# Attention, layer norm and two MLPs in one planned order: later landings and dearer POOL handovers in the planner, layer norm sums as float32r products

## The chip, the core and the metric

The kernel runs on one core of one Trainium2 chip. The core has a matrix engine (PE, with its weight loads, PEld), a vector engine (DVE), an activation engine (ACT), a general engine (POOL) and a queue that issues DMAs (SP). The metric is the device time in microseconds of one execution; lower is better. Float32r is the single-pass form in which PE reads 4-byte operands; a plain float32 product takes several passes.

## The reference, cut to what matters

```python
# attention per head: softmax(scale*q.k + min(bias from a cumulated s, 0), causal) @ v
x = attn_out.transpose(0, 2, 1, 3).reshape(B, S, H * D)          # B=4, S=576, 512 columns
mu = np.mean(x, axis=-1, keepdims=True)
var = np.mean((x - mu) ** 2, axis=-1, keepdims=True)
xn = (x - mu) / np.sqrt(var + 1e-06) * g_ln
x = x + np.maximum(xn @ w_ch1, 0.0) @ w_ch2                      # first MLP, 512 -> 2048 -> 512
u = x + ((x.transpose(0, 2, 1) @ U) @ V).transpose(0, 2, 1)      # mixing over the sequence, rank 32
out = u + np.maximum(u @ w2_ch1, 0.0) @ w2_ch2                   # second MLP
```

## The kernel before, in words

The work is cut into blocks: each of the four batches has a block A (256 positions) and a block B (320) for attention, layer norm and the first MLP, in the order A0 A1, A2 A3, B0, B1, B2, B3. The second MLP goes over C0, C1, C2 (512 positions of a batch each), T0 (the last 64 positions of all four batches) and C3. Nearly all products are float32r with operands split into a high and a low part, three products for one: L1396 to L1398 are the first half of the first MLP (and of T0), L1453 to L1455 its second half, L1309 to L1311 and L1347 to L1349 the two halves for C blocks. L765, L769 and L747 are attention's scores, L773 and L752 their reductions on DVE, L823 the transposes, L867 and L896 attention's second product. L1244 mixes T0's positions, one batch at a time.

Nothing is issued in the order of the text. Every step is recorded by `P.op` with its engines, a duration on each of them and its buffers, and `Plan.plan` places the steps one by one, earliest start first, on a model of the engines. What the model uses: `HOP`, the time from one engine's end to another's start; a DMA rate (350 bytes per ns) with 1500 ns from the queue's end to the reader, to which a load may add a `lag`; pools of buffers (`ps` six and `acc` two PSUM banks, `xs` two, `ls` four, `pB` two); and priorities from the tables `AT` (when a block's attention is spread over the MLP steps), `LN` (its layer norm), `W0`, `W1` (conversion of the second MLP's weights from 64-bit words) and `HEAD`. `Plan.issue` plans once from those priorities and then up to `PASSES` times from due times, and issues the order with the earliest planned end. Each engine then executes its own list strictly in that order, waiting on semaphores. So a step whose input comes later than the model says holds up everything behind it on its engine.

Where the plan leaves PE idle before the first MLP step, `issue` puts fillers there (L1603), short products into a bank that nobody reads.

The layer norm of a block (all but A0 and A1, which normalise by rows) sums over the 512 features, which lie on the partitions and in four tiles: `ln_sum` adds the four tiles (L386 on DVE or L388 on POOL, as the plan chooses) and then multiplies with a matrix of 1/512 to sum over the partitions and to spread the mean to all of them (L967). It is called twice a block, for the mean and for the variance:

```python
ps = psum()
pe(prio - 500, 4 * mm_cost(n), lambda: nc.tensor.matmul(ps[:, :n], ones.tile, into[:, :n], start=True, stop=True), [ones, into], [ps])
return ps
```

`split` takes a source and writes its high part (a copy with rounding to float32r, `copy`, on ACT or DVE: L381, L382) and its low part (source minus high part, `tt`, on DVE or POOL: L386, L388).

Of the kernel before, what the change touches and what calls it, by code (L numbers as in the profile page):

```python
# [10 lines left out]
F32R = mybir.dt.float32r  # L11
I32 = mybir.dt.int32
U32 = mybir.dt.uint32
AF = mybir.ActivationFunctionType
# [17 lines left out]
LAST = ("C0", "C1", "C2", "T0", "C3")  # L32
W2SLOTS = 12

AT = {"A2": (1, 3), "A3": (1, 33), "B0": (26, 49), "B1": (50, 65), "B2": (67, 83), "B3": (83, 100)}
LN = {"A2": 9, "A3": 33, "B0": 62, "B1": 66, "B2": 84, "B3": 102}
W0 = (1, 14)
HEAD = {-100: -1, -50: 127, 1.5: 61, 4.5: 18, -4: 1, -3: -8}
W1 = (16, 60, 59)
PASSES = 4  # L40
AHEAD = 1500


def f(ap):
    return ap.bitcast(F32)


def mm_cost(n):
    return max(106.7, n / 2.4) + 13.3


HOP = {
    ("pe", "act"): 200, ("pe", "dve"): 200, ("act", "pe"): 290, ("dve", "pe"): 285, ("pool", "pe"): 200,
    ("act", "dve"): 150, ("dve", "act"): 200, ("act", "act"): 150, ("dve", "dve"): 130, ("pool", "pool"): 100,
    ("act", "pool"): 170, ("dve", "pool"): 180, ("pool", "act"): 80, ("pool", "dve"): 80, ("pe", "pe"): 60,
}


# [30 lines left out]
class Plan:  # L89
# [196 lines left out]
    def issue(self, warm):  # L286
# [9 lines left out]
        for _ in range(PASSES):  # L296
            prio = self.latest(order, end)
            for o in self.ops:
                prio[o.seq] -= 1e3 * HEAD.get(o.prio, HEAD.get(o.prio + 500, 0))
            use = {e: [0.0] * NW for e in price}  # L300
# [35 lines left out]
def mha_ffn_mixer_ffn(ctx: ExitStack, tc, qkv_p, qkv_a, qkv_b, s, g, w1, w2, U, V, out):  # L336
    nc = tc.nc
    P = Plan(nc)
# [20 lines left out]
    def psum():  # L359
        return P.buf("ps", [128, 512])  # L360
# [6 lines left out]
    def act(prio, n, fn, reads, writes, fixed=94):  # L367
        P.op(prio, {"act": (fixed + 0.8333 * n, fn)}, reads, writes)

    def pe(prio, cost, fn, reads, writes, hold=()):  # L370
        return P.op(prio, {"pe": (cost, fn)}, reads, writes, hold=hold)
# [2 lines left out]
        return 4 * max(n / 2.4, 53.3) + 2.5  # L374

    def load(prio, nbytes, fn, reads, writes, gate=None, rate=350.0, lag=0):
        P.op(prio, {"sp": (475, fn)}, reads, writes, nbytes, gate, rate=rate, lag=lag)

    def copy(prio, n, out, a, reads, writes, psum=False, soft=0.0, slow=False):
        P.op(prio, {  # L380
# [10 lines left out]
    def split(prio, n, hi, lo, src, reads, wh, wl, psum=False, soft=0.0, slow=False):  # L391
        copy(prio, n, hi, src, reads, wh, psum, soft, slow)
        tt(prio, n, lo, src, lambda: f(hi()), ALU.subtract, list(reads) + list(wh), wl, psum, soft)


    def fixed(name, shape, dtype=F32):
        return P.fixed(const.tile(shape, dtype, name=name))

    ident = fixed("ident", [128, 128])
    ones = fixed("ones", [128, 128])  # L400
    eps = fixed("eps", [128, 1])
    odd = fixed("odd", [128, 1])
    g_sb = fixed("g_sb", [128, KT])
    small = fixed("small", [128, 4])
# [14 lines left out]
    PRO = -1e6  # L419

    def setup():
# [14 lines left out]
            dve(PRO, 1, lambda a=a, z=z: nc.vector.memset(odd[a:a + R], z), [], [(odd, "y%d" % a)])  # L436
        dve(PRO, 128, lambda: nc.vector.memset(ones.tile, 1.0 / DM), [], [ones], 0.521)
        P.op(PRO, {"pool": (600, lambda: nc.gpsimd.memset(causal.tile, 0.0))}, [], [causal])
        for y in range(4):
            act(PRO, R, lambda y=y: nc.scalar.activation(sel[R * y:R * (y + 1)], ident[R * y:R * (y + 1), R * y:R * (y + 1)], AF.Copy),  # L440
                [ident, table], [(sel, "y%d" % y)])
# [131 lines left out]
    def w2_ahead(m, gate):  # L573
        prio = NS0 + m - 8
        raw, t = w_raw(prio, 1, m, 1, gate, AHEAD), psum()
        f64_to_f32(prio, 512, lambda: t.tile, lambda: raw.tile, t, raw, psum=True)
# [3 lines left out]
    def w1_ahead(p, gate):  # L580
        prio, dr = NS0 + 2 * p - 9, w1_dr[p]
        raws, ts = [], []
        for z in range(2):
            raw, t = w_raw(prio, 1, 2 * p + z, 0, gate, AHEAD), psum()
            f64_to_f32(prio, 512, lambda t=t: t.tile, lambda raw=raw: raw.tile, t, raw, psum=True)
# [31 lines left out]
    class Pair:  # L617
# [94 lines left out]
        def bias(self, prio, tick, gate):  # L712
# [5 lines left out]
            for y in range(2):  # L718
                load(prio, 256 * S, lambda t=t, y=y: nc.sync.dma_start(
                    t[64 * y:64 * (y + 1)], cum_dr[idx + y:idx + y + 1].to_broadcast([64, S])), [cum_dr], [(t, "y%d" % y)], gate, 260.0, AHEAD // 2)  # L720
                d = lambda y=y: t[64 * y:64 * (y + 1), 512:S]
# [239 lines left out]
    def ln_sum(prio, n, srcs, reads, into):  # L961

        for k in range(1, KT):
            tt(prio, n, lambda: into[:, :n], srcs[0] if k == 1 else lambda: into[:, :n], srcs[k], ALU.add,
               (reads[0] if k == 1 else [into]) + reads[k], [into])
        ps = psum()
        pe(prio - 500, 4 * mm_cost(n), lambda: nc.tensor.matmul(ps[:, :n], ones.tile, into[:, :n], start=True, stop=True), [ones, into], [ps])  # L967
        return ps

    def layer_norm(prio, b, blk):  # L970
# [530 lines left out]
    for m in range(MT):  # L1501
        at = W1[0] + W1[1] * m / 8 if m < 8 else W1[0] + W1[1] + W1[2] * (m - 8) / 8
        if m % 2 == 0:
# [18 lines left out]
    for st in range(NS0, NS, 2):  # L1522
        _, _, blk, m = steps[st]
# [25 lines left out]
    put(start1 - 12, lambda p, g: mix_prep_v(p, g))  # L1549
    for x in AT:  # L1550
        b, blk = int(x[1]), x[0]
        if x not in FULL:
            for p, pr in enumerate(pairs_of[b, blk]):
                put(max(0, AT[x][0] - 6 + p), lambda p, g, pr=pr: pr.bounce(p, g))
        spread(attn_items(b, blk), *AT[x])
        put(LN[x], lambda p, g, b=b, blk=blk: layer_norm(p, b, blk))
    for (l, b, blk), p in final.items():
# [95 lines left out]
```

## Time and profile before

| what | value |
|---|---|
| median of 3 runs | 1037.3 us (1037.26 to 1037.39) |
| the profiled execution | 1036.19 us, span from first to last instruction 1034.4 us |
| granted TensorE clock | 1.0 of full speed, over the whole span |
| PE busy | 1017.1 us, 98% of the span |
| DVE, ACT, POOL busy | 694.6, 470.2, 138.5 us |
| DMA | 248.80 MB in the span, mean 241 GB/s |

The busy share of an engine counts the recorded instructions; the ends of matmuls are modelled, so that neighbours overlap in the records and the time that one matmul really takes is the distance from its start to the next one's.

### The profile page before, as it was taken

The numbers are of one execution on the slowest core, as the hardware profiler recorded it, in microseconds if no ns is written. First come the engines' busy times: TensorE is split into PE (matmuls) and PEld (weight loads), VectorE is DVE, ScalarE is ACT, GpSimd is POOL, SyncE is SP. The second block draws the span as 40 slices with busy tenths as digits, with TensorE's granted clock in tenths as the row PEclk, the third lists the DMA queues.
The fourth block names the chain that finished last, engine by engine and source line by source line (L and its number), as shares of the span: only waits on it lengthen the run. The fifth ranks groups of instructions, "written<-read, shape, count | busy, mean of one in ns | idle before, by whom it ended". The sixth has DMA issues, their size and how long they took to land.

```text
span 1034.4 us, 19312 instructions
## 1 busy us (share of the span) xinstructions
PE 1017.1 (98%) x7110; PEld 938.8 (91%) x7110; DVE 694.6 (67%) x1760; ACT 470.2 (45%) x1104; POOL 138.5 (13%) x288
## 2 busy tenths in 40 slices
PE   8999999999999999989999999999999999999998
PEld 7888888999999999979999999898999899899897
DVE  7999989866988878678754428547446645517444
ACT  6889877755856556557543314312111211112110
POOL 0021333511620222032100000001001000001000
PEclk9999999999999999999999999999999999999999
DMA  8999984668656976595475799981763576487851
GB/s 296 342 339 344 335 310 145 212 228 295 215 165 201 305 245 218 181 315 184 128 286 205 248 394 358 348 321 46 266 217 106 198 240 191 143 287 235 316 172 42
DMA packets 99231, 248.80 MB, mean 241 GB/s; under 512 B 16416, under 2 KB 47392, under 8 KB 94528
## 3 DMA queue, kind: packets, MB, share of 16 engines
q1 hardware_dynamic: 98464, 246.97, 69.6%
q8 instruction: 56, 0.92, 0.4%
q10 hardware_dynamic: 672, 0.59, 0.2%
q14 instruction: 39, 0.32, 0.1%
HBM read 193.97 MB, written 62.99 MB: 248 GB/s over the span
## 4 chain that ended last, share of the span: by engine, by line
PE 77%; DVE 5%; DMA 2%; ACT 2%; issue 1%; SPq 0%; DVEq 0%; POOL 0%; ACTq 0%; POOLq 0%
PE ps L1396 6%; PE ps L1398 5%; PE ps L1397 5%; PE ps L1309 5%; PE ps L1311 5%; PE ps L1310 5%; PE ps L867 4%; PE acc L1453 4%; PE acc L1454 4%; PE acc L1455 4%; PE ps L823 3%; PE acc L1347 3%; PE acc L1349 3%; PE acc L1348 3%; PE ps L1347 3%; PE ps L1348 3%
## 5 line engine op out<-in xcount | busy, mean ns | idle before, releaser
L1396 PE MATMUL ps<-xh,w 128*128 128x256 f32 (+1 forms) x512 | 157.8, 308 | 1.8 <-DVE pB L386 0.9
L1398 PE MATMUL ps<-xl,w 128*128 128x256 f32 (+1 forms) x512 | 151.3, 295 | 0.0
L1397 PE MATMUL ps<-xh,w 128*128 128x256 f32 (+1 forms) x512 | 151.2, 295 | 0.0
L1403 DVE SCALAR_TENSOR_TENSOR hl<-ps,hh 128x256 fp32r<-128x256 f32 (+1 forms) x144 | 64.5, 449 | 94.4 <-ACT hh L1402 94.0
L1402 ACT ACTIVATE hh<-ps 128x256 fp32r<-128x256 f32 (+1 forms) x144 | 58.2, 404 | 119.1 <-PE ps L1398 118.4
L1396 PEld LDWEIGHTS ps<-xh,w 128*128 128x128 f32 x512 | 96.7, 189 | 9.1 <-DVE pB L386 1.6
L1397 PEld LDWEIGHTS ps<-xh,w 128*128 128x128 f32 x512 | 96.8, 189 | 2.2
L1453 PE MATMUL acc<-hh,w 128*128 128x256 f32 (+1 forms) x320 | 97.3, 304 | 0.0
L1398 PEld LDWEIGHTS ps<-xl,w 128*128 128x128 f32 x512 | 96.6, 189 | 0.0
L1454 PE MATMUL acc<-hh,w 128*128 128x256 f32 (+1 forms) x320 | 93.8, 293 | 0.0
L1455 PE MATMUL acc<-hl,w 128*128 128x256 f32 (+1 forms) x320 | 93.8, 293 | 0.0
L1269 ACT ACTIVATE w<-hl 128x256 fp32r<-128x256 f32 x83 | 34.1, 418 | 124.7 <-DVE hl L1289 124.5
L783 ACT ACTIVATE t<-t,mx 128x384 f32<-128x384 f32 (+4 forms) x112 | 68.9, 617 | 47.0 <-DVE mx L773 39.2
L1289 DVE TENSOR_TENSOR hh<-ps,hh 128x256 f32<-128x256 f32 x64 | 27.1, 423 | 77.7 <-ACT hh L381 76.1
L1289 DVE TENSOR_TENSOR hl<-ps,hh 128x256 f32<-128x256 f32 x128 | 48.6, 419 | 44.9 <-PE ps L1311 43.7
L381 ACT ACTIVATE hh<-ps 128x256 f32<-128x256 f32 x31 | 12.0, 386 | 113.9 <-PE ps L1311 113.7
L386 DVE TENSOR_TENSOR pB<-ps,pB 128x384 fp32r<-128x384 f32 (+2 forms) x112 | 60.0, 569 | 5.2 <-ACT pB L381 4.7
L773 DVE CUSTOM_DVE_ANT_0 t<-ps,causal 128x128 f32<-128x128 f32 (+3 forms) x128 | 56.9, 484 | 8.5 <-PE ps L769 8.1
L1453 PEld LDWEIGHTS acc<-hh,w 128*128 128x128 f32 x320 | 60.7, 190 | 1.5 <-issue 1.0
L1454 PEld LDWEIGHTS acc<-hh,w 128*128 128x128 f32 x320 | 60.7, 190 | 0.5
L1455 PEld LDWEIGHTS acc<-hl,w 128*128 128x128 f32 x320 | 60.6, 190 | 0.0
L1295 DVE SCALAR_TENSOR_TENSOR w<-hl,w 128x256 fp32r<-128x256 f32 x128 | 52.3, 426 | 6.6 <-ACT w L1269 5.7
(258 smaller groups left out, 2894.8 us busy)
## 6 DMA issues: line engine op xcount, KB each, us to landing
w<-w_dr SPq DMA_DIRECT2D x112, 512.0 KB, 7.3
pB<-w_dr SPq DMA_DIRECT2D x36, 1024.0 KB, 5.4
qk<-w_dr SPq DMA_DIRECT2D x28, 768.0 KB, 5.2
w_dr<-w SPq DMA_DIRECT2D x32, 512.0 KB, 6.0
w_dr<-wr SPq DMA_DIRECT2D x32, 512.0 KB, 4.8
wr<-w1a SPq DMA_DIRECT2D x16, 512.0 KB, 6.3
wr<-w2a SPq DMA_DIRECT2D x16, 512.0 KB, 6.2
wr<-w1b SPq DMA_DIRECT2D x16, 512.0 KB, 6.5
```

Of the source, the lines that this page charges most:

```text
L386: alts = {"dve": (68 + 1.042 * n, lambda: nc.vector.tensor_tensor(out=out(), in0=a(), in1=b(), op=op))}
L783: act(prio, K, lambda t=t, mx=mx, o=o, K=K, x=x, y=nt * z + x: nc.scalar.activation(t[:, o:o + K], t[:, o:o + K], AF.Exp, bias=mx[:, (1 if ...
L1289: dve(st - 1000, 256, lambda: nc.vector.tensor_tensor(out=d.tile, in0=region(r), in1=a.tile, op=ALU.add), [p, a], [d])
L1347: nc.tensor.matmul(aa[z].tile, w[:, 0, sl], h[:, 0], start=first, stop=False)
L1348: nc.tensor.matmul(aa[z].tile, w[:, 1, sl], h[:, 0], start=False, stop=False)
L1396: nc.tensor.matmul(ps[:, :n], lhs(k, 0), xh[:, k, :n], start=k == 0, stop=False)
L1397: nc.tensor.matmul(ps[:, :n], lhs(k, 1), xh[:, k, :n], start=False, stop=False)
L1398: nc.tensor.matmul(ps[:, :n], lhs(k, 0), xl[:, k, :n], start=False, stop=k == KT - 1)
L1403: dve(st - 1000, n, lambda: nc.vector.scalar_tensor_tensor(out=hl[:, :n], in0=ps[:, :n], scalar=0.0, in1=f(hh[:, :n]), op0=ALU.max, op1=AL ...
L1453: nc.tensor.matmul(a, w[:, 0, sl], hh[:, :n], start=new, stop=False)
L1454: nc.tensor.matmul(a, w[:, 1, sl], hh[:, :n], start=False, stop=False)
L1455: nc.tensor.matmul(a, w[:, 0, sl], hl[:, :n], start=False, stop=last and (z == 1 or blk == "B"))
```

## The change

Three things change in the text. The planner takes every load with a priority above zero (all but those of the prologue and of the first block) to be read 1000 ns later than before (`LATE`); `HOP` from POOL to PE, ACT and DVE is 500 ns instead of 200, 80 and 80. The sum over partitions in `ln_sum` becomes a split of the added tile into two float32r parts and two float32r products with a float32r copy of the 1/512 matrix. And the tables `AT`, `LN`, `W0`, `HEAD` and `W1` have new numbers. Below line 400 the lines of the changed kernel stand a little further down: L967 becomes L975, L1396 L1407, L1244 L1255, L773 L776, L1463 L1474, L1603 L1614.

```diff
-AT = {"A2": (1, 3), "A3": (1, 33), "B0": (26, 49), "B1": (50, 65), "B2": (67, 83), "B3": (83, 100)}
+AT = {"A2": (1, 3), "A3": (1, 33), "B0": (26, 49), "B1": (46, 65), "B2": (69, 83), "B3": (83, 100)}
...
-W1 = (16, 60, 59)
+W1 = (16, 66, 56)
...
+LATE = 1000
...
-    ("pe", "act"): 200, ("pe", "dve"): 200, ("act", "pe"): 290, ("dve", "pe"): 285, ("pool", "pe"): 200,
+    ("pe", "act"): 200, ("pe", "dve"): 200, ("act", "pe"): 290, ("dve", "pe"): 285, ("pool", "pe"): 500,
...
-    ("act", "pool"): 170, ("dve", "pool"): 180, ("pool", "act"): 80, ("pool", "dve"): 80, ("pe", "pe"): 60,
+    ("act", "pool"): 170, ("dve", "pool"): 180, ("pool", "act"): 500, ("pool", "dve"): 500, ("pe", "pe"): 60,
...
-        P.op(prio, {"sp": (475, fn)}, reads, writes, nbytes, gate, rate=rate, lag=lag)
+        P.op(prio, {"sp": (475, fn)}, reads, writes, nbytes, gate, rate=rate, lag=max(lag, LATE if prio > 0 else 0))
...
+    mean_w = fixed("mean_w", [128, 128], F32R)
...
+        act(PRO + 1, 128, lambda: nc.scalar.activation(mean_w.tile, ones.tile, AF.Copy), [ones], [mean_w])
...
         ps = psum()
-        pe(prio - 500, 4 * mm_cost(n), lambda: nc.tensor.matmul(ps[:, :n], ones.tile, into[:, :n], start=True, stop=True), [ones, into], [ps])
+
+        parts = [P.buf("ls", [128, 320], F32R) for _ in range(2)]
+
+        def mm():
+            for z, a in enumerate(parts):
+                nc.tensor.matmul(ps[:, :n], mean_w.tile, a[:, :n], start=z == 0, stop=z == 1)
+
+        split(prio, n, lambda: parts[0][:, :n], lambda: parts[1][:, :n], lambda: into[:, :n], [into], [parts[0]], [parts[1]])
+        pe(prio - 500, 2 * mm_cost(n), mm, [mean_w] + parts, [ps])
         return ps
```

Over the whole program PE has the same matmuls in both orders, but for the 12 layer norm products, which become 24, and the fillers, 54 before and 60 now. Of the 12 new splits the order gives 10 high parts to ACT and 2 to DVE. Additions and subtractions that write an `ls` tile: 17 on POOL before, 27 now. The order of every engine is cut anew; three places follow.

**DVE, where the attention of B3 begins beside the layer norm of B2.** `v0` is the tile of the values, `xs0` the raw values that a DMA brings, the `ISA` rows on t0 and t1 the reductions of scores, which free `ps4` and `ps1` (before) or `ps0` and `ps4` (now). Before:

```order
L386 TENSOR_TENSOR xc0_6642<-xc0_6642,ls0_6728 128x320
L382 CAST xh0_6801<-xc0_6642 128x320
L382 CAST v0_6710<-xs0_6726 128x5x64
L386 TENSOR_TENSOR xl0_6806<-xc0_6642,xh0_6801 128x320
L386 TENSOR_TENSOR v0_6710<-xs0_6726,v0_6710 128x5x64
L773 ISA t0_6789,mx4_6815<-ps4_6787,causal_91 128x512
```

Of the change, the same reductions and, 24 rows further on, the same cast:

```order
L776 ISA t0_6812,mx4_6835<-ps0_6810,causal_92 128x512
L776 ISA mx4_6835 128x1
L776 ISA t1_6813,mx5_6846<-ps4_6811,causal_92 128x512
...
L755 ISA t2_6822,mx0_6942<-ps0_6852,t2_6822,mx0_6942 128x288
...
L383 CAST v0_6844<-xs0_6914 128x5x64
L1414 SCALAR_TENSOR_TENSOR hl2_6961<-ps4_6959,hh2_6960 128x320
```

The cast that waits for the landing stood ahead of the reductions and now stands behind them, and behind those of the pair's last scores (t2).

**DVE, where C0 begins.** The rows of x3 add B3's finished MLP to x and free the two accumulators and two `ps` banks; `wr` are tiles of the second MLP's weights in conversion. Before:

```order
L1463 TENSOR_TENSOR x3_7041<-x3_7041,acc0_8421 128x320
L534 SCALAR_TENSOR_TENSOR ps3_9066<-ps3_9066,wr1_8963 128x512
L1463 TENSOR_TENSOR x3_7041<-x3_7041,ps2_8422 128x320
L382 COPY wr2_9103<-ps3_9066 128x256
L386 TENSOR_TENSOR wr3_8943<-ps1_9041,wr3_8943 128x512
L1289 TENSOR_TENSOR hh1_9115<-ps4_9056,hh0_9054 128x256
L1463 TENSOR_TENSOR x3_7041<-x3_7041,acc1_8459 128x320
L1289 TENSOR_TENSOR hl2_9118<-ps4_9056,hh1_9115 128x256
L1463 TENSOR_TENSOR x3_7041<-x3_7041,ps0_8460 128x320
```

Of the change:

```order
L1474 TENSOR_TENSOR x3_7209<-x3_7209,acc0_8468 128x320
L387 TENSOR_TENSOR xs1_9121<-x1_8890,xs0_9045 128x512
L1300 TENSOR_TENSOR hh0_9131<-ps1_9062,hh2_9109 128x256
L383 CAST xh1_9139<-xs1_9121 128x512
L1474 TENSOR_TENSOR x3_7209<-x3_7209,ps4_8469 128x320
L387 TENSOR_TENSOR xh1_9139<-xs1_9121,xh1_9139 128x512
L1474 TENSOR_TENSOR x3_7209<-x3_7209,acc1_8494 128x320
L1300 TENSOR_TENSOR hh1_9165<-ps2_9123,hh0_9131 128x256
L1474 TENSOR_TENSOR x3_7209<-x3_7209,ps3_8495 128x320
```

The conversions of `wr` have left the stretch between the four additions; they come later in C0.

**PE, where T0 begins.** L1244 (now L1255) is the mixing of the fourth batch, with the operand t5 (now t3); L1347 to L1349 (now L1358 to L1360) are second-half products of C2; L1396 (now L1407) is T0's first product. Before, the last two mixing rows and on:

```order
L1244 MATMUL ps0_11719<-t0_8631,t5_11707 128x64
L1244 MATMUL ps0_11719<-t1_8642,t5_11707 128x64
L1347 MATMUL acc0_10984<-w0_11595,w1_11096 128x512
L1348 MATMUL acc0_10984<-w0_11595,w1_11096 128x512
...
L1348 MATMUL ps3_10999<-w0_11595,w1_11096 128x512
L1349 MATMUL ps3_10999<-w0_11595,w1_11096 128x512
L1396 MATMUL ps1_11751<-wr1_11735,pB0_11555 128x256
```

Of the change:

```order
L1359 MATMUL ps5_11067<-w5_11655,w9_11224 128x512
L1360 MATMUL ps5_11067<-w5_11655,w9_11224 128x512
L1255 MATMUL ps3_11818<-t0_8692,t3_11803 128x64
L1255 MATMUL ps3_11818<-t1_8696,t3_11803 128x64
...
L1407 MATMUL ps1_11838<-wr1_11829,pB0_11621 128x256
L1408 MATMUL ps1_11838<-wr1_11829,pB0_11621 128x256
```

Twelve products of C2 stood between the last mixing and T0's first product and none does now; between the third and the fourth mixing there were 6, and are 24 now. The low part of the fourth operand was made by DVE and is now made by POOL, and on SP the load for it stands behind one of T0's weight loads instead of ahead of it.

## Rows read from the trace of the kernel before

**Rows 1.** The page: busy time by engine; the chain that ended last.

```profile
PE 1017.1 (98%) x7110; PEld 938.8 (91%) x7110; DVE 694.6 (67%) x1760; ACT 470.2 (45%) x1104; POOL 138.5 (13%) x288
...
PE 77%; DVE 5%; DMA 2%; ACT 2%; issue 1%; SPq 0%; DVEq 0%; POOL 0%; ACTq 0%; POOLq 0%
```

**Rows 2.** Stretches: length, then busy PE, PEld, DVE, ACT, POOL; clock; DMA.

```profile
0.00:40.00 40.00, 35.79 (x292) 29.42 (x293) 33.52 (x136) 30.48 (x74) 2.13 (x12) 1.00 0.90 312
...
100.00:200.00 100.00, 97.92 (x713) 87.22 (x712) 90.77 (x234) 79.51 (x204) 35.18 (x66) 1.00 0.73 253
200.00:440.00 240.00, 239.70 (x1813) 228.06 (x1813) 187.54 (x471) 146.29 (x332) 56.52 (x132) 1.00 0.70 229
440.00:460.00 20.00, 17.08 (x119) 14.90 (x115) 14.76 (x36) 11.15 (x27) 8.62 (x17) 1.00 0.95 327
...
620.00:640.00 20.00, 18.68 (x132) 18.14 (x131) 15.91 (x31) 9.01 (x17) 1.30 (x1) 1.00 1.00 382
...
880.00:920.00 40.00, 37.88 (x273) 35.29 (x272) 16.24 (x38) 6.42 (x15) 0.00 (x0) 1.00 0.59 200
...
1020.00:1034.40 14.40, 10.49 (x55) 8.48 (x53) 5.68 (x17) 0.42 (x1) 0.00 (x0) 1.00 0.21 73
```

**Rows 3.** PE's waits, longest first: total us, times, longest.

```profile
PE ps L747 <- DVE mx L773: 2.0, 1, 2.0
...
PE ps L1309 <- DVE x L1463: 1.3, 1, 1.3
PE ps L1396 <- DMA pB<-w_dr: 1.3, 1, 1.3
...
PE ps L1396 <- DVE pB L386: 0.9, 1, 0.9
PE ps L1244 <- DVE t L386: 0.8, 1, 0.8
```

**Rows 4.** PE in time around one layer norm product: start, length, instruction.

```profile
331.36 0.70 PE L967 MATMUL ps<-ls,ones 128*128 128x320 f32 x2
331.66 0.55 PE L1453 MATMUL acc<-hh,w 128*128 128x320 f32 x1
332.04 0.31 PE L1454 MATMUL acc<-hh,w 128*128 128x320 f32 x1
332.19 0.31 PE L1455 MATMUL acc<-hl,w 128*128 128x320 f32 x1
```

**Rows 5.** SP, DVE and POOL in time, 437 to 447 us.

```profile
437.59 0.33 SPq L661 DMA_DIRECT2D xs<-qkv_b  x1
...
444.47 0.49 DVE L382 CAST v<-xs 128x320 fp32r<-128x320 f32 x1 [2.15 <-POOL xs L663]
...
445.39 1.10 POOL L388 TENSOR_TENSOR xc<-xc,ls 128x320 f32<-128x320 f32 x1
...
445.70 1.14 DVE L386 TENSOR_TENSOR v<-xs,v 128x320 fp32r<-128x320 f32 x1
446.76 0.68 DVE L773 CUSTOM_DVE_ANT_0 t<-ps,causal 128x512 f32<-128x512 f32 x1
```

**Rows 6.** DVE in time where C0 begins.

```profile
635.66 0.70 DVE L534 SCALAR_TENSOR_TENSOR ps<-ps,wr 128x512 uint32<-128x512 uint32 x1
...
639.02 0.48 DVE L1463 TENSOR_TENSOR x<-x,ps 128x320 f32<-128x320 f32 x1
```

**Rows 7.** DVE in time behind the fourth mixing of T0.

```profile
892.24 0.42 DVE L1247 TENSOR_TENSOR wr<-wr,ps 128x256 f32<-128x256 f32 x1 [0.71 <-PE ps L1244]
892.69 0.50 DVE L382 CAST wr<-wr 128x256 fp32r<-128x256 f32 x2
```

**Rows 8.** Groups by shape: xcount | busy us, mean ns | idle before.

```profile
L388 POOL TENSOR_TENSOR ls<-ls,ls 128x320 f32<-128x320 f32 x1 | 0.9, 883 | 3.3 <-ACT ls L981 3.3
...
L386 DVE TENSOR_TENSOR ls<-ls,ls 128x320 f32<-128x320 f32 x11 | 5.3, 484 | 0.1
```

**Rows 9.** PE in time, fillers before the first MLP step.

```profile
20.66 2.13 PE L1603 MATMUL acc<-ones 128*128 128x256 bf16 x18
```

More of the change, by code (lines that the diff above doesn't have):

```diff
@@ L33 @@
 W2SLOTS = 12
-AT = {"A2": (1, 3), "A3": (1, 33), "B0": (26, 49), "B1": (50, 65), "B2": (67, 83), "B3": (83, 100)}
-LN = {"A2": 9, "A3": 33, "B0": 62, "B1": 66, "B2": 84, "B3": 102}
-W0 = (1, 14)
-HEAD = {-100: -1, -50: 127, 1.5: 61, 4.5: 18, -4: 1, -3: -8}
-W1 = (16, 60, 59)
+AT = {"A2": (1, 3), "A3": (1, 33), "B0": (26, 49), "B1": (46, 65), "B2": (69, 83), "B3": (83, 100)}
+LN = {"A2": 9, "A3": 33, "B0": 63, "B1": 66, "B2": 84, "B3": 106}
+W0 = (1, 16)
+HEAD = {-100: -1, -50: 125, 1.5: 61, 4.5: 33, -4: 1, -3: -8}
+W1 = (16, 66, 56)
 PASSES = 4
 AHEAD = 1500
+LATE = 1000
 def f(ap):
```

## Prediction

> **What bounds the kernel now.** I read the page first. PE is busy 98% of the span and the chain that ended last runs over PE for 77% of it, with DVE next at 5% [rows 1]. PE is the bound, so the time is PE's own work plus whatever PE waits; the other engines matter only where they make it wait. The span is 1034.4 us and PE's busy time 1017.1, so 17.3 us are idle. The stretches tell where [rows 2]: 40 - 35.79 = 4.2 us in the first 40 us, 2.1 between 100 and 200, 2.9 between 440 and 460, 1.3 between 620 and 640, 2.1 between 880 and 920, and 3.9 in the last 14.4 us, most of it behind the last product. That is 16.5 of the 17.3; the long stretches between lose almost nothing. PE's waits name the events in the middle [rows 3]: 2.0 us for DVE's score reductions, 1.3 for DVE's addition L1463, 1.3 for a landing of `pB`, 0.9 for DVE's `pB`, 0.8 for a `t`.
>
> The profiled execution took 1036.2 us, 1.1 less than the median of 1037.3; differences worked out in its rows are put on the median.
>
> **Layer norm products.** What a float32 product costs is read from PE's starts [rows 4]. L967's first record starts at 331.36, the next engine's work at 331.66: 0.30 us. That next product then runs 0.38 us to its successor (332.04) where the one after takes 0.15 (332.19 - 332.04), so 0.23 of L967 is still in the array. One product of 320 columns costs 0.30 + 0.23 = 0.53 us. Two float32r products of 320 columns cost 2 x 0.147 = 0.29 by the same rows. Saved: 0.24 us, eight times (two sums in each of four B blocks), 1.9 us. The four products of 256 columns I scale by columns, an estimate: 0.19 each, 0.8 us. **Term: -2.7 us.** All 12 stand between products of the MLP with no idle time beside them, so it is PE's own time; bounds -2.2 to -2.9.
>
> The price is 12 splits, 12 copies and 12 subtractions. A 320-column addition in `ls` takes 0.484 us on DVE and 0.883 on POOL [rows 8]. The norm of a block is planned well ahead of its MLP (by the table `LN`, B1's at step 66, while B1's MLP begins at step 80, and 14 steps are 14 x 24 products of 0.147 us, some 49 us), so the longer chain of some 2 us a norm, two copies and two subtractions, is covered. What is not covered is DVE's time between 100 and 200 us, where it is busy 90.8 of 100 us [rows 2] and where the norms of A2 and A3 lie: by the order DVE gets 3 more `ls` operations of 256 columns there, 0.39 us each scaled from 0.484, 1.2 us. **Term: +0.3**, nearer to nothing because PE idles only 2.1 us there although DVE is that full; bounds 0 and +1.2.
>
> **Landings.** `LATE` and `HOP` change no transfer; they change what is put in front of what. At 437.59 SP issues a load of `xs`; DVE waits 2.15 us with the cast that reads it until 444.47; the score reduction behind the cast starts at 446.76 [rows 5], and PE needs the bank that it frees: the wait of 2.0 us [rows 3]. In the new order that cast stands 24 rows behind the same reductions, and behind those of the next scores. A landing just as late then holds up nothing that PE needs soon. **Term: -2.0**, and of the 0.9 us that PE waits a little later for DVE's backlog, half: **-0.5**. Bounds 0 and -2.9.
>
> **Where C0 begins.** PE's 1.3 us end with the last of the four L1463 at 639.02 [rows 6], which frees a bank. Before it stood two conversions (L534, 0.70 each) with their copy and subtraction, some 2.5 us. The new order has none of these there. **Term: -1.3**, bounds 0 and -1.3. They come later in C0, where DVE has slack (15.9 of 20 us even in the full stretch).
>
> **Where T0 begins.** Two waits go: the 0.8 us for the `t` (24 products of C2, not 6, now stand ahead of the fourth mixing) and perhaps the 1.3 for `pB`, because more second-half products of T0 are placed before each new weight tile. One comes: nothing of C2 is left between the fourth mixing and T0's first product. From the addition's start at 892.24 to the first cast's end at 892.69 + 0.25 is 0.7 us [rows 7]; with handovers of 0.2 to 0.3 at both ends and the low parts arriving one by one I take 1.5 us. The fourth operand is also made by POOL, with its load behind 1 MB of weights: +0.4. Together -2.1 + 1.9 = **-0.2**; bounds -2.1 (all covered) and +2.5.
>
> **The head.** Six more fillers at 2.13 / 18 = 0.12 us [rows 9] are 0.7 us of PE. They fill waiting that the plan expects; I take **+0.4**, bounds -1.0 and +1.5, since the 4.2 idle us of the head depend on an order that is new throughout. The copy for `mean_w` (one ACT operation) ends long before the first norm.
>
> **The rest of the order** is cut anew as well. I put its other waits at what they were, **0**, bounds -2 and +3.
>
> Sum: -2.7 + 0.3 - 2.5 - 1.3 - 0.2 + 0.4 + 0 = -6.0 us. The profiled execution would take 1030.2 us, the median **1031.3**.
>
> **A rule weighed.** DVE's subtraction at 445.70 took 1.14 us, beside a POOL addition that started at 445.39 and took 1.10 [rows 5]; a DVE addition of that size alone takes 0.484 [rows 8]. So 0.66 us of DVE were lost to POOL. The Trainium skill (SBUF — State Buffer, Who interferes with whom) says that DVE, with two inputs in SBUF, and a POOL instruction that reads SBUF exclude each other for a whole instruction; that row agrees. By that rule the change is worse than it looks, since it moves additions to POOL. What it would give is the second rival.
>
> **Rivals.**
> *The waits only move.* The plan is blind to what it was blind to before, and the 9 us that PE idles between head and tail come back at other places. Against it stand the two places in DVE's order at which the cause is seen to be gone. Then only the norm products (-2.7) and the fillers (+0.7) remain: 1035.3 us.
>
> *POOL holds DVE (slower).* POOL gets 27 of the `ls` operations instead of 17. Ten more at 0.66 us of DVE each are 6.6 us. If DVE passes all of that to PE, and the waits of the landings return elsewhere, the time is 1037.3 - 2.7 + 6.6 = 1041.2. It is slower by more than 0.2% from the point where 4.8 of these 6.6 us reach PE (2.7 gained, 2.1 for the 0.2%). For it: the score reductions behind such a held DVE row made PE wait. Against it: between 200 and 440 us DVE is busy 187.5 of 240 us and PE idle 0.3 [rows 2], so DVE has room there.
>
> *T0's beginning costs its upper bound.* The fourth operand comes 2.7 us later than I take it: 1031.3 + 2.7 = 1034.0, still faster.
>
> **How the numbers follow.** About 0.2% (2 us) is what a measurement here can tell from no change. Chances: the forecast with its bounds 0.60, T0's late beginning 0.10, waits that only move 0.16, POOL holding DVE or as much lost otherwise 0.14. The second last gives 1035.3, at the edge of 2 us. So faster 0.70, within 0.2% 0.16, slower 0.14. Adding all good ends (-2.9 - 2.9 - 1.3 - 2.1 - 1.0 - 2) gives 1025.1, all bad ones (-2.2 + 1.2 + 2.5 + 1.5 + 3) 1043.3; neither is likely in all its terms at once. I take 1026.0 to 1039.0, which leaves out the tip of the good side and the worst of the POOL case. Within the forecast alone it is 1027.5 to 1034.5.
>
> **What will show it.** Layer norm: two records of about 0.15 us pitch and no slow successor. Landings: no wait of L747 (now L750) near 440 us; if DVE still idles there for `xs`, but PE does not, the step is right. C0: no wait for L1474. T0: a new wait of 1 to 2 us of L1407 for DVE or ACT right behind L1255. Head: PE's idle time in the first 40 us within 1.5 us of 4.2. The prediction is wrong if PE's idle time between 40 and 1020 us stays at the 9.2 us of before (17.3 - 4.2 - 3.9), or if the head loses more than 2 us.

## The result and the profile after

The changed kernel takes 1026.2 us (median of 4 runs, 1025.4 to 1027.1), the kernel before 1037.3 beside it: a ratio of 0.9892, 95% interval 0.9875 to 0.9909, so 11.1 us or 1.1% faster. The forecast was 1031.3. The sign was right, and PE lost most of its idle time at the places that were named; the size was half of what came. The 1026.2 lie at the very edge of the stated range (1026.0 to 1039.0) and outside the 1027.5 to 1034.5 that the forecast alone allowed.

In the profiled execution the span falls from 1034.4 to 1024.3 us. The page of the changed kernel, busy time by engine and the chain that ended last (as [rows 1]):

```profile
PE 1013.0 (99%) x7116; PEld 937.3 (92%) x7116; DVE 691.4 (67%) x1763; ACT 476.3 (47%) x1122; POOL 146.8 (14%) x292
...
PE 86%; DVE 7%; DMA 4%; ACT 2%; issue 1%; POOLq 0%; SPq 0%; DVEq 0%; ACTq 0%; POOL 0%
```

PE's busy time fell by 1017.1 - 1013.0 = 4.1 us and its idle time from 17.3 to 1024.3 - 1013.0 = 11.3, by 6.0. Stretches as in [rows 2] (length, then busy PE, PEld, DVE, ACT, POOL; clock; DMA), the last one from 920 us on:

```profile
0.00:40.00 40.00, 36.62 (x311) 30.63 (x312) 35.25 (x139) 33.70 (x82) 2.13 (x12) 1.00 0.94 332
...
100.00:200.00 100.00, 99.06 (x740) 89.15 (x739) 87.93 (x232) 76.15 (x199) 34.46 (x62) 1.00 0.76 257
200.00:440.00 240.00, 238.64 (x1799) 226.08 (x1798) 190.22 (x474) 152.44 (x352) 60.29 (x137) 1.00 0.65 217
440.00:460.00 20.00, 20.00 (x143) 19.45 (x142) 15.68 (x42) 13.68 (x32) 5.21 (x11) 1.00 0.98 332
...
620.00:640.00 20.00, 19.85 (x141) 18.72 (x141) 19.97 (x46) 11.50 (x23) 1.67 (x1) 1.00 0.76 276
...
880.00:920.00 40.00, 38.60 (x300) 37.12 (x299) 10.26 (x25) 5.97 (x15) 1.29 (x1) 1.00 0.68 246
920.00:1020.00 100.00, 99.79 (x654) 90.76 (x653) 51.06 (x128) 16.07 (x37) 3.07 (x2) 1.00 0.53 188
```

PE's idle time (length less busy time), before and after: 4.2 and 3.4 us in the head, 2.1 and 0.9 from 100 to 200, 0.3 and 1.4 from 200 to 440, 2.9 and none from 440 to 460, 1.3 and 0.15 where C0 begins, 2.1 and 1.4 where T0 begins. Of these only the one from 200 to 440 grew, and 0.2 us came behind 920. PE's waits (as [rows 3]):

```profile
PE acc L1614 <- DVE ones L439: 1.5, 1, 1.5
PE ps L1407 <- DVE wr L383: 0.8, 1, 0.8
PE ps L1407 <- DVE hl L1414: 0.6, 1, 0.6
PE ps L1407 <- DVE mx L776: 0.5, 1, 0.5
PE ps L1407 <- DMA pB<-w_dr: 0.5, 1, 0.5
PE ps L768 <- DVE w L387: 0.5, 1, 0.5
```

Behind the start (1.5, as before) nothing is longer than 0.8 us, and that one is the new wait at T0's beginning which the prediction announced. The waits of 2.0, 1.3, 1.3 and 0.9 us of [rows 3] are gone, or 0.5. Between the head and the tail, PE idles some 4 us (0.9 + 1.4 + 0.15 + 1.4 + 0.2) where it idled 9.2.

### The profile page after: what moved, and what is told of

Same layout as the page of the kernel before. It is cut to its first block, busy times and chain, and to the rows that moved or that the text cites. A ratio compares the mean times of both kernels' runs of the same rounds, so it can differ in the third digit from the quotient of the medians.

```text
span 1024.3 us, 19382 instructions
## 1 busy us (share of the span) xinstructions
PE 1013.0 (99%) x7116; PEld 937.3 (92%) x7116; DVE 691.4 (67%) x1763; ACT 476.3 (47%) x1122; POOL 146.8 (14%) x292
## 4 chain that ended last, share of the span: by engine, by line
PE 86%; DVE 7%; DMA 4%; ACT 2%; issue 1%; POOLq 0%; SPq 0%; DVEq 0%; ACTq 0%; POOL 0%
PE ps L1407 7%; PE ps L1409 7%; PE ps L1408 7%; PE ps L1320 5%; PE ps L1322 5%; PE ps L1321 5%; PE ps L870 4%; PE acc L1464 4%; PE acc L1466 3%; PE acc L1465 3%; PE ps L826 3%; PE acc L1358 3%; PE acc L1359 3%; PE acc L1360 3%; PE ps L1358 3%; PE ps L1359 3%
## 5 line engine op out<-in xcount | busy, mean ns | idle before, releaser
L1407 PE MATMUL ps<-xh,w 128*128 128x256 f32 (+1 forms) x512 | 158.0, 309 | 1.9 <-DVE hl L1414 0.6
L1407 PEld LDWEIGHTS ps<-xh,w 128*128 128x128 f32 x512 | 96.6, 189 | 10.4 <-issue 2.8
L776 DVE CUSTOM_DVE_ANT_0 t<-ps,causal 128x256 f32<-128x256 f32 (+3 forms) x128 | 56.4, 485 | 10.8 <-PE ps L772 10.5
```

Of the source, the lines that this page charges most:

```text
L1407: nc.tensor.matmul(ps[:, :n], lhs(k, 0), xh[:, k, :n], start=k == 0, stop=False)
```

## The experiments

Twelve kernels ran. Each ratio is to the kernel before on the same chip; the changed kernel's own is 0.9892. The last column is the median.

| kernel | ratio (95%) | us |
|---|---|---|
| after_ln_fp32 | 0.9907 (0.9894 to 0.9920) | 1026.8 |
| after_no_ln | 1.0057 (1.0042 to 1.0071) | 1042.8 |
| after_no_late | 1.0083 (1.0063 to 1.0102) | 1043.8 |
| after_old_hop | 1.0051 (1.0037 to 1.0065) | 1041.4 |
| before_cast | 0.9993 (0.9982 to 1.0005) | 1035.7 |
| before_c0 | 1.0015 (1.0003 to 1.0026) | 1038.1 |
| before_lnr | 0.9986 (0.9972 to 1.0000) | 1034.7 |
| before_three | 1.0005 (0.9990 to 1.0019) | 1036.6 |
| before_far | 0.9994 (0.9976 to 1.0012) | 1036.4 |
| after_ls_dve | 0.9952 (0.9934 to 0.9970) | 1032.6 |
| after_late990 | 0.9894 (0.9875 to 0.9914) | 1026.9 |
| after_old_tables | 0.9935 (0.9916 to 0.9953) | 1030.7 |

The medians of before beside them were 1036.4 to 1036.9.

Where two kernels have the same order on PE, their records can be laid side by side, each with the same instruction of the other. The table gives how much later (us) PE starts the instruction that the first of the two starts at the time in the head line; each from one profiled execution of either.

| later than | kernel | 40 | 100 | 200 | 300 | 440 | 520 | 620 | 660 | 880 | 920 | 1015 |
|---|---|---|---|---|---|---|---|---|---|---|---|---|
| changed | after_ln_fp32 | 1.7 | 1.7 | 1.6 | 1.1 | 1.6 | 1.5 | 2.0 | 2.0 | 2.0 | 1.2 | 1.2 |
| changed | after_ls_dve | 2.2 | 2.2 | 3.6 | 6.1 | 7.0 | 7.3 | 7.3 | 7.3 | 7.3 | 6.5 | 6.5 |
| before | before_cast | 0.2 | -0.4 | 0.3 | 0.2 | 1.0 | 0.2 | 0.2 | 0.2 | 0.2 | 0.5 | 0.5 |
| before | before_c0 | -1.3 | -1.6 | -1.7 | -1.7 | -1.5 | -2.3 | -2.3 | 0.6 | 0.6 | 0.2 | 0.2 |
| before | before_lnr | -0.9 | -1.0 | -0.7 | -0.7 | -0.1 | -0.3 | -0.8 | -1.1 | -1.1 | -0.5 | -0.5 |
| before | before_three | -1.3 | -1.8 | -1.1 | -1.4 | 1.4 | -0.6 | -1.1 | 1.7 | 1.7 | 1.0 | 1.0 |
| before | before_far | -0.6 | -1.1 | -0.8 | -1.0 | -0.4 | -2.0 | -2.5 | 0.7 | 0.8 | -0.5 | -0.5 |

None of these kernels changes anything in the first 40 us but for a small operation that makes weights (before_lnr, before_three, before_far). So the head differs by up to 2 us from one execution to the next, and an edit is read from the step at its own place. Steps of some 0.9 us come without any edit: before_c0 changes nothing between 440 and 520 us, and PE gains 0.9 there.

### The price of the products: after_ln_fp32 and before_lnr

Both keep the order of all engines. after_ln_fp32 goes back to float32 in the changed kernel:

```diff
-            for z, a in enumerate(parts):
-                nc.tensor.matmul(ps[:, :n], mean_w.tile, a[:, :n], start=z == 0, stop=z == 1)
+            a = parts[0]
+            nc.tensor.matmul(ps[:, :n], ones.tile, f(a[:, :n]), start=True, stop=True)
```

> Changed kernel with its order kept row for row on DVE, ACT, POOL and SP, but each pair of float32r products of the layer norm sums replaced by one float32 product of the high part alone (the low part of the sums is left out). So only PE's price of the sums is changed back. By the term of the prediction (0.53 us for a float32 product of 320 columns against 0.29 for the pair, eight times, and 0.19 us for each of four of 256 columns): 2.7 us slower than the changed kernel, 1028.9 us, bounds 2.2 to 2.9. Rival: the products lie where PE would wait anyway, so that their price is not PE's own time: 0 to 1 us slower.

Around one of the sums, PE in time, start, length and instruction; first the changed kernel:

```profile
428.61 0.46 PE L975 MATMUL ps<-ls,mean_w 128*128 128x320 f32 x2
428.90 0.31 PE L1464 MATMUL acc<-hh,w 128*128 128x320 f32 x1
429.05 0.31 PE L1465 MATMUL acc<-hh,w 128*128 128x320 f32 x1
```

then after_ln_fp32:

```profile
429.65 0.70 PE L975 MATMUL ps<-ls,ones 128*128 128x320 f32 x2
429.95 0.56 PE L1464 MATMUL acc<-hh,w 128*128 128x320 f32 x1
430.35 0.30 PE L1465 MATMUL acc<-hh,w 128*128 128x320 f32 x1
```

The pair takes 428.90 - 428.61 = 0.29 us. The float32 product takes 0.30 and delays its successor to 0.40 where 0.15 is the pitch: 0.55 in all. That is the prediction's reading of [rows 4], measured again. PE's busy time is 1015.1 us, 2.1 more than in the changed kernel. But from 100 to 620 us, where all the sums lie, PE falls back by only 2.0 - 1.7 = 0.3 us, and the medians differ by 0.5 (the ratios by 1.5, with intervals that overlap; by the ratios alone the 2.7 of the term are not excluded). The changed kernel waits where this run does not: the waits of 0.6 for `hl` and 0.5 for `mx` in the list above are not in this run.

before_lnr does the opposite in the kernel before, without the splits:

```diff
-        pe(prio - 500, 4 * mm_cost(n), lambda: nc.tensor.matmul(ps[:, :n], ones.tile, into[:, :n], start=True, stop=True), [ones, into], [ps])
+        def mm():
+            for z in range(2):
+                nc.tensor.matmul(ps[:, :n], mean_w.tile, into[:, :n], start=z == 0, stop=z == 1)
+
+        pe(prio - 500, 4 * mm_cost(n), mm, [ones, into], [ps])
```

> Kernel before with its order kept, but each layer norm sum's float32 product made two float32r products of the sum rounded to float32r (the sums are rounded at each addition and there is no low part, so no split on DVE or POOL; one extra DVE operation at the start makes the weights). This is PE's price of the change alone. By the term of the prediction: 2.7 us faster than before, bounds 2.2 to 2.9. By the run of the changed kernel with float32 products, which cost it far less than 2.7 (medians 0.5 apart, ratios 1.5): 0.5 to 1.6 us faster, because a part of the time given back is spent waiting for DVE a little later.

The ratio of 0.9986 is 1.5 us (0 to 2.9), which does not exclude the term either. The records show where the time goes. Laid beside the kernel before, PE gains 0.2 to 0.3 us at each of the eight sums of 320 columns and some 0.2 at each of the four of 256, as the prediction priced them. It gives 1.6 us back between 346 and 353 us, where it now idles 0.6 + 0.4 us for DVE (none before), and the rest in smaller steps: between 40 and 880 us it gains 0.1.

```profile
345.86 0.66 PE L753 MATMUL ps<-qk 128*128 128x288 f32 x3 [0.60 <-DVE mx L779]
353.09 1.15 PE L829 MATMUL ps<-ident,t 128*128 128x128 f32 x6 [0.41 <-DVE mx L758]
```

### Two rows moved by hand: before_cast, before_c0, before_three, before_far

These keep the order of the kernel before and move a few operations (numbered as they are made) behind a later one, with whatever between depends on them. before_cast:

```diff
+        for names, goal in [((2605, 2606), 2614)]:
+            k = next(i for i, c in enumerate(best) if c[0].seq == goal)
+            late = [i for i, c in enumerate(best) if c[0].seq in names]
+            moved = set()
+            for i in range(min(late), k + 1):
+                o = best[i][0]
+                if o.seq in names or any(d.seq in moved for d in o.deps) or any(d.seq in moved for d in o.slots):
+                    moved.add(o.seq)
+            best = ([c for c in best[:k + 1] if c[0].seq not in moved] + [c for c in best[:k + 1] if c[0].seq in moved] + best[k + 1:])
```

> Kernel before with its order kept, but two DVE rows moved: the cast and the subtraction that wait for the landing of xs near 440 us stand behind the two score reductions (and behind the next 1/sum, an ls subtraction and an hl) instead of ahead of them. Theory of the prediction: 2.0 to 2.9 us faster than before, no wait of L747 near 440. Rival (PE waits for the next thing): the wait goes, but a new one near it takes its place, 0 to 1 us faster.

Less than the theory's 2.0 us is gained (the interval ends at 1.9), as the rival had it. By the records it is 0.75 us between 440 and 520, no more than before_c0 gains there without an edit. In before_cast (lines numbered 10 higher than before), DVE in time near 440 us:

```profile
444.56 0.69 DVE L783 CUSTOM_DVE_ANT_0 t<-ps,causal 128x512 f32<-128x512 f32 x1 [0.75 <-PE ps L779]
...
448.29 0.47 DVE L392 CAST v<-xs 128x320 fp32r<-128x320 f32 x1
...
451.47 0.46 DVE L762 CUSTOM_DVE_ANT_0 t<-ps,t 128x288 f32<-128x288 f32 x1 [0.78 <-DMA t<-cum_dr]
```

and PE's waits there:

```profile
450.38 0.52 PE L833 MATMUL ps<-ident,t 128*128 128x128 f32 x3 [0.78 <-DVE rc L802]
453.21 1.09 PE L833 MATMUL ps<-ident,t 128*128 128x128 f32 x8 [1.43 <-ACT t L808]
454.77 0.41 PE L1406 MATMUL ps<-xh,w 128*128 128x320 f32 x1 [0.47 <-DVE pB L396]
```

The reductions start 2.2 us earlier than the 446.76 of [rows 5], and the wait of 2.0 is gone. PE then runs into the next landing: the reduction L762 waits until 451.47 for `t` from `cum_dr`, the softmax's `t` is late by as much, and PE idles 0.78 + 1.43 + 0.47 = 2.7 us in the stretch, 2.9 before. In the kernel before, SP issues those two loads of `t` from 440.45 on, and in before_cast from 441.79. In the changed kernel SP issues them at 434.21, and the first of those reductions runs at 446.57, without a wait. So in this run the next late results, one of them a landing, take the place of the one whose row DVE waited in.

before_c0 has `[((3366, 3369, 3362), 3524)]` in the same place.

> Kernel before with its order kept, but three DVE rows moved: the conversion L534, its copy and the subtraction that stand between the four L1463 where C0 begins now stand behind the last of them. Theory of the prediction: 1.3 us faster than before, no wait of L1309 for L1463 over 0.2 us. Rival: C0 then waits for the converted weights instead, 0 to 0.5 us faster.

It is 1.6 us slower by the ratio (0.3 to 2.7), so both theory and rival were wrong. By the records PE is 2.3 us ahead at 620 us, up to which nothing is changed, and loses 2.9 between 620 and 660. PE in time:

```profile
636.70 0.39 PE L1319 MATMUL ps<-xc,pB 128*128 128x256 f32 x1 [0.79 <-DVE x L1473]
...
639.33 0.47 PE L1319 MATMUL ps<-xl,qk 128*128 128x256 f32 x1 [1.66 <-DVE hl L1299]
```

The wait for the addition shrank from 1.3 to 0.8; behind it PE now waits 1.7 us for C0's `hl`, in front of which the conversions stand, 0.66 us of that while DVE waits for ACT's half of a conversion. And the granted clock fell (stretch, busy PE, PEld, DVE, ACT, POOL, clock, DMA):

```profile
639.00:643.00 4.00, 3.67 (x18) 3.67 (x19) 3.59 (x11) 1.44 (x4) 0.00 (x0) 0.57 0.61 229
```

0.43 of 4 us is another 1.7 us of PE.

before_three has both moves and the products of before_lnr; before_far has the products and further moves, `[((2714,), 2682), ((2605, 2606), 2634), ((3366, 3369, 3362), 3512)]`.

> Kernel before with the three edits together: the cast behind the reductions, the conversion behind the four additions, float32r products of rounded sums; the rest of the order as before. If the terms add up as the prediction has them: 2.7 + 2.5 + 1.3 = 6.5 us faster than before, about 1030.3. Rival (waits move): less than the sum of the three single runs by over 1 us.

> Kernel before with float32r products of rounded sums and the two moves made far enough: near 440 us the cast and subtraction that wait for xs stand behind the next 1/sum (the load that reuses their buffer moves behind them), and one weight load on SP stands behind the two loads of the next scores' t; where C0 begins, the conversions stand behind four more operations of C0's hidden layer. All else keeps its place. Theory (each wait can be taken away if what lands late has nothing behind it): the waits between 440 and 460 us fall from 2.9 to under 1 us, those between 620 and 640 to under 0.5, and the run is 3 to 6 us faster than before. Rival (waits only move): it stays where the float32r products alone put it, 0 to 2 us faster than before, with the idle time of the two stretches no smaller.

Neither is measurably faster than before, and the theories (6.5 and 3 to 6 us faster) are outside both intervals. By the records the two places go apart in both. Between 440 and 520 us before_far gains 1.6 us and before_three 1.9. The weight load that before_far moves behind the loads of `t` is not what does it: before_three has the cast where before_cast has it and DVE still waits 1.2 us for `t` there. PE's wait there falls from 2.0 us to 1.4 (before_three) and 1.6 (before_far), and is one for ACT's `t` now.

before_three loses most where none of its moves lies, 3.9 us between 340 and 360. Its PE comes earlier by the products and meets another landing of `xs`, with the same row behind it as at 440; the kernel before does not wait here. DVE, then PE:

```profile
343.95 0.49 DVE L392 CAST v<-xs 128x320 fp32r<-128x320 f32 x1 [0.98 <-POOL xs L679]
346.22 0.68 DVE L789 CUSTOM_DVE_ANT_0 t<-ps,causal 128x512 f32<-128x512 f32 x1
346.96 1.09 PE L763 MATMUL ps<-qk 128*128 128x288 f32 x3 [2.46 <-DVE mx L789]
```

The clock then falls (0.51 from 347 to 350). At C0 both lose: before_three 2.8 us between 620 and 660, before_far 3.2. In before_far the idle time from 620 to 640 is 0.8 us, less than before, but PE idles longer right behind it, for the next `hl` in front of which the conversions now stand, and the clock falls again (these lines stand 21 higher than before; the PE row, then the stretch behind it):

```profile
642.12 0.65 PE L1144 MATMUL ps<-ident,x 128*128 128x128 f32 x4 [1.77 <-DVE hl L1310]
```

```profile
642.00:646.90 4.90, 4.78 (x21) 4.27 (x22) 4.66 (x15) 2.33 (x6) 0.00 (x0) 0.65 0.51 150
```

So near 440 us the move wins something in two of three runs and never the whole wait; that it is the landings together that hold PE there is the likely reading, not a shown one. At C0 the row that the prediction blamed is only one of several that DVE has to do before PE can go on, and moving it puts it in front of the next.

### The margins: after_no_late, after_old_hop, after_late990, after_old_tables, after_no_ln

Here the order is cut anew. The edits:

```diff
-LATE = 1000
+LATE = 0
```

in after_no_late, 990 in after_late990;

```diff
-    ("pe", "act"): 200, ("pe", "dve"): 200, ("act", "pe"): 290, ("dve", "pe"): 285, ("pool", "pe"): 500,
+    ("pe", "act"): 200, ("pe", "dve"): 200, ("act", "pe"): 290, ("dve", "pe"): 285, ("pool", "pe"): 200,
...
-    ("act", "pool"): 170, ("dve", "pool"): 180, ("pool", "act"): 500, ("pool", "dve"): 500, ("pe", "pe"): 60,
+    ("act", "pool"): 170, ("dve", "pool"): 180, ("pool", "act"): 80, ("pool", "dve"): 80, ("pe", "pe"): 60,
```

in after_old_hop. after_old_tables has the five tables of before (`AT`, `LN`, `W0`, `HEAD`, `W1`), after_no_ln the layer norm sums of before.

> Changed kernel with LATE = 0, all else kept; the order is cut anew. Theory (the later landing keeps casts that wait for loads out of DVE's way): the waits that were lost at 440 us and at T0's weight tile come back here or elsewhere, 2.5 us slower, about 1028.7, and at least one wait of PE over 1 us ends with DVE work that itself waited for a DMA. Rival (the gain came with the tables, the margin does nothing by itself): within 1 us of 1026.2.

> Changed kernel with the old HOP values (0.08 and 0.2 us behind POOL instead of 0.5), all else kept; the order is cut anew. Theory (the margin keeps POOL's late results out of what PE needs): 1 to 3 us slower, 1027 to 1029, with waits of PE behind POOL results. Rival (POOL holds DVE, and the margin changes only who gets the work): follows the count of layer norm additions on POOL, here 18 rows instead of 27, so 0 to 6 us faster than 1026.2.

> Changed kernel with LATE = 990 in place of 1000: the same margins as near as can be, tables and layer norm kept, but the order is cut anew (some 300 of DVE's 1715 rows stand elsewhere). Theory (the margins carry the gain): within 2 us of the changed kernel, 1025 to 1028. Rival (the order that these tables give with exactly these margins carries it): 1030 to 1042, with waits of PE at places where the changed kernel has none.

> Changed kernel with the old intervals (AT, LN, W0, HEAD, W1), margins and layer norm kept; the order is cut anew. Theory (the margins carry the gain): 1027 to 1031, since landings and POOL results are still assumed late. Rival (the tables were fitted to one order): 1034 to 1044, like the three runs that left out another part.

> Changed kernel with the layer norm's part taken out (one float32 product, no splits), margins and tables kept; the order is cut anew. By the terms (products 2.7, splits on DVE 0.3 the other way): 2.4 us slower than the changed kernel, about 1028.7. Rival (the tables fit one order, and any new cut of it loses): clearly more, 1031 to 1035, with new waits of PE that have nothing to do with the layer norm.

Measured: 1043.8, 1041.4, 1026.9, 1030.7 and 1042.8 us. For the two margins the sign is the theory's, the size is far beyond it: 15 to 18 us. In after_no_ln it is beyond both theory and rival. A margin of 990 is as good as one of 1000, though the order differs: 178 of DVE's 1603 planned steps and 59 of PE's 1228 stand outside the longest order that the two plans share. With the old intervals but both margins and the products, the kernel is 6.7 us (0.65%) faster than before; the new intervals add the other 4.5.

What a margin does is read from DVE's waits (what waits, for what; us in total, times, longest). Before:

```profile
DVE rc L792 <- POOL sm L790: 9.9, 14, 1.4
...
DVE v L382 <- POOL xs L663: 3.1, 2, 2.1
DVE qk L382 <- DMA qk<-qkvB: 2.5, 3, 1.5
```

The changed kernel:

```profile
DVE rc L795 <- POOL sm L793: 5.5, 7, 1.3
DVE qk L383 <- DMA qk<-qkvB: 4.4, 5, 1.6
```

after_old_hop, the margin behind POOL alone taken away:

```profile
DVE rc L795 <- POOL sm L793: 13.7, 18, 1.3
DVE qk L383 <- DMA qk<-qkvB: 2.4, 1, 2.4
```

The reciprocal `rc` waits for POOL's `sm`; with the margin, other rows are put ahead of it. Added over all its rows, DVE waits for POOL 5.1 to 7.8 us in the seven kernels with that margin, and 10.9 to 15.6 in the seven without it: this margin cuts the wait that it is about. For the landings it is not shown. DVE waits for DMA 8.7 us before and 10.5 in after_no_late, and 7.0, 5.7 and 6.0 in the changed kernel, after_late990 and after_old_tables; but it is 10.3 in after_no_ln, which has the margin, and 6.5 in before_far, which has not, and the wait for `qk` above grew. (The 3.1 us for POOL's `xs` before are landings too: POOL's row waits for the DMA.) Both together are 17.3 to 23.3 us in all nine kernels that take over 1034 us, and 11.0 to 12.7 in all five that take under 1033. Within either set they do not go with the time: before_far has 17.3 at 1036.4 us and after_no_late 18.3 at 1043.8.

Nor are PE's longest waits those of the margin that was taken away. In after_no_late the three longest are 1.95 us behind two DVE subtractions that take 2.42 us beside POOL's work, 1.59 behind a `rc` that waited 1.66 for POOL, and 1.53 for POOL itself; of the five over 1 us, one ends with DVE work that had waited for a DMA (0.55 us), where the theory wanted at least one. In after_old_hop the longest, 1.71, stands behind a landing:

```profile
383.22 0.36 DVE L383 CAST qk<-qk 128x384 fp32r<-128x384 f32 x1 [2.40 <-DMA qk<-qkvB]
```

Part of the size is the new cut itself. The planner of each kernel, run without the chip, gives the end that it plans: 1021.4 us for the changed kernel, 1024.1 for after_no_late, 1025.5 for after_old_hop and 1030.3 for after_no_ln, so 2.7, 4.1 and 9.0 us are lost in the plan already, although the first two assume less delay. The measured time is 4.9 us more than planned in the changed kernel, 6.0 and 8.7 in after_late990 and after_old_tables, and 12.5 in after_no_ln; without one margin or both it is 15.9 to 19.7 (17.1 before). So a plan with both margins comes nearer to what it promises. after_no_ln also has seven waits of PE of 0.65 to 1.72 us between 140 and 280 us and one of 1.0 at 521, all for DVE. after_old_hop gives DVE 708.1 us of work instead of 691.4, and more work on DVE costs time by itself (the next run). How much of the 15 to 18 us is the missing margin alone, these runs can't tell.

### POOL's share: after_ls_dve

```diff
+            if e == "pool" and "dve" in o.alts and any(b.tag == "ls" for b in o.bufs):
+                e = "dve"
```

> Changed kernel with its order kept, but every layer norm row that POOL does (27 sums and low parts, 8 products by 1/sigma) done by DVE at its place. Rival of the prediction (POOL holds DVE): as DVE is freed of POOL's reads, 0 to 3 us faster than the changed kernel. Theory (POOL's rows cost nothing, since DVE has room where they stand): DVE gets 35 rows of 0.39 to 0.48 us, some 15 us in all, and the time rises by 0 to 3 us with new waits of PE for DVE between 100 and 440 us.

It is 6.3 us slower than the changed kernel (1032.6 against 1026.2; by the ratios 0.0060, 6.2 us), twice what the theory had. By the records 5.1 us come between 100 and 520, where the rows lie; 2.2 lie in the head, where nothing is changed, and 0.8 come back at T0. PE's waits between 100 and 440 us (lines 2 higher than in the changed kernel):

```profile
PE ps L1023 <- DVE x L1436: 1.5, 1, 1.5
...
PE ps L1409 <- DVE mx L778: 0.9, 1, 0.9
...
PE ps L1149 <- DVE xs L389: 0.7, 1, 0.7
```

The first two were 0.4 and 0.5 in the changed kernel. The rival of the prediction is refuted for this order, with its sign reversed: POOL's 35 rows are worth some 5 us in an order that was planned with them. The ten more rows of the rival are also only three: POOL's rows that write or read `ls` tiles are 35 now and were 32 before.

## Why the prediction was right in sign and half in size

**Layer norm products, -2.7.** The price on PE is right: 0.55 against 0.29 us, 2.1 us of PE's busy time by after_ln_fp32, and 0.2 to 0.3 us at each sum of before_lnr. The step that failed is "All 12 stand between products of the MLP with no idle time beside them, so it is PE's own time". By the medians and ratios of two experiments the products are worth 0.5 to 2.1 us of the time (with intervals that reach past 2.7), by the records 0.1 to 0.3, since PE gives the rest back in the waits that come next.

**100 to 200 us, +0.3.** Wrong sign: PE idles 1.1 us less there. The added rows are there: DVE has 16 rows that write or read `ls` tiles (8.9 us) instead of 10 (5.3). But DVE is busy 87.9 us in all instead of the 90.8 of [rows 2], and POOL and ACT are less busy too, so other work has moved out of this stretch, which the prediction did not count. What POOL's rows keep off DVE, after_ls_dve puts at 1.4 us between 100 and 200 and at 3.7 from there to 520.

**Landings, -2.0 and -0.5.** PE's 2.9 us near 440 are gone, a little more than the term. But "A landing just as late then holds up nothing that PE needs soon" is not enough: before_cast makes this move, and before_three and before_far too, and PE still idles 1.9 to 2.7 us between 440 and 460. The changed order also has the loads of `t` 6 us earlier on SP and all of its rows anew; which of that took the rest away is not shown.

**C0, -1.3.** 1.3 - 0.15 = 1.2 us of idle time went, so the size is right. The reason is not: "They come later in C0, where DVE has slack" failed in before_c0 and before_far. In the changed kernel DVE is busy 19.97 of these 20 us; it does other work there and does not wait.

**T0, -0.2.** It was -0.7. The uncovered chain came as described and costs 0.84 us, not 1.5; the wait for `t` is gone and that for `pB` is 0.5.

**Head, +0.4, and the rest, 0.** The head's idle time is 0.8 us less in this execution, within what it varies by (4.1 in after_ln_fp32, which has the same head). The rest of the order costs 1.1 from 200 to 440 us and 0.2 behind 920, and gains 0.4 from 40 to 100.

So the idle time fell by 6.0 us where the prediction's terms for it sum to -4.0 (+0.3 - 2.5 - 1.3 - 0.2, and -0.3 in the head, which is its +0.4 less 0.7 of fillers), and PE's busy time by 4.1 where they sum to -2.0 (-2.7 + 0.7). Of the 2.0 us of idle time that were missed, 1.4 lie between 100 and 200 us. Of the 4.1 us, 2.1 are the products by after_ln_fp32 and 0.3 the fillers (8.7 us by their starts in place of 9.9, of which 0.2 and 1.1 are idle time behind them); 1.7 is not traced. The difference of the medians is 1 us more than that of the spans, since the profiled execution of before lay 1.1 below its median. That the total still fell into the range is in part luck: the products were taken for more than they gave, and the other terms for less.

There is an error of method too: the prediction priced a new order by the waits whose row had moved. What the margins and intervals do all along the order was left at 0, as "the rest". With the margins, the products and the old intervals the kernel is 6.7 us faster, near the forecast by its number; the new intervals, which the prediction priced only at the places where it saw rows move, give 4.5 more. What the margins give apart from a new cut is not shown: no run has the products and the old intervals without them, or them alone. Of the rivals, "the waits only move" is what most hand moves do in the old order (before_cast, before_c0 and the earlier PE of before_lnr). In the changed order most of the waits are gone.

**The rule weighed.** The Trainium skill (SBUF — State Buffer, Who interferes with whom) says that DVE with two SBUF inputs and a POOL instruction that reads SBUF exclude each other. The rows agree again: in before_far DVE's subtraction of `v` at 448.09 takes 1.50 us, beside a POOL product of 1.03 from 448.20. But "By that rule the change is worse than it looks" did not hold: a DVE row that is held by POOL now and then costs less than POOL's rows on DVE, by some 5 us. It is not free: the longest wait of PE in after_no_late stands behind two DVE rows that were held so.

## What to carry to other kernels

Where an order is planned ahead, moving the one row that waits is seldom enough: the next late result of the same stretch takes its place, or the moved row stands in front of the next one that matters. A plan that takes landings and a slow engine's results as later came nearer to its promise here (5 to 13 us off instead of 16 to 20); how much of the gain is the margins' own was not separated. Time taken off the bounding engine is partly given back as waiting (2.1 us of PE were worth 0.5 to 2.1, by the records still less), and rows taken off a full engine that it waits for are worth time themselves (POOL's rows some 5 us). Intervals that suit one plan need not suit another: with any one of three parts of the change taken out, the new intervals left the kernel slower than it was before the change.

## What the runs showed of the hardware

A PE wait can cost more than its length. Behind 0.79 + 1.66 us of idle time from 635.9 to 639.3, the granted clock of before_c0 is 0.50 (1.2 GHz) from 640 to 642 us, and 1.7 us more are lost; in before_far the same, 1.7 us, behind 1.77. Nine such falls lie in the middle of these profiles (two in before_three and two in after_no_ln, one each in before_c0, before_far, after_late990, after_no_late and after_old_hop), and each costs 1.7 us. It is not the length of the wait alone: the wait of 1.98 us of [rows 3] left the clock at 1.0 in the profile of before, as did 2.2 at the same place in before_lnr, and in after_late990 1.3 us of idle time were enough for it at 888 us. The runs of before beside before_cast show it as spread: the 11 runs with a mean clock of 1.0 took 1036.6 us in the mean, the 4 with 0.997 took 1038.5. At equal clock (1.0) the hand moves come out at -0.9 (before_cast), +0.6 (before_c0) and -1.6 us (before_three), and before_lnr at -1.7, from four to seven runs each, which changes no verdict above.
